# The same normalisation in another order of steps, and new slots around it, in a gated linear-attention and Fourier-mixing kernel

## The chip, the cores and the metric

The kernel runs on one core of a Trainium2 chip. The metric is the device time of one execution in microseconds (us). TensorE (PE) multiplies matrices, VectorE (DVE) and ScalarE (ACT) do the element-wise work, GpSimd (POOL) and SyncE (SP) mostly issue transfers (DMAs). Each of the five engines has its own queue of instructions and works it off in order.

## The reference, cut to what matters

x has 2048 rows and 576 columns; there are 32 heads of 18 columns.

```python
S, D, H, Dh = 2048, 576, 32, 18
g = sigmoid((x * gate_w).sum(-1, keepdims=True))
q, k, v = the three parts of x @ wqkv, by heads
phi = lambda t: where(t > 0, t + 1, exp(t)) + 1e-6
kv  = einsum("bhsd,bhse->bhde", phi(k), v)
z   = einsum("bhsd->bhd", phi(k))
num = einsum("bhqd,bhde->bhqe", phi(q), kv)
den = einsum("bhqd,bhd->bhq", phi(q), z)[..., None] + 1e-6
a   = (num / den) joined over heads, @ wo
b   = dft_seq_re @ (x @ dft_hid_re.T) - dft_seq_im @ (x @ dft_hid_im.T)
out = g * a + (1 - g) * b
```

## The kernel before

All products are made in pairs of numbers: a rounded part ("hi", written by ACT, `hi_of`) and what the rounding left ("lo", the remainder, a subtraction by DVE, `lo_of`), so that one float32 product is three matmuls. Rows are in 16 tiles of 128. The large products go by a seven-product scheme on 2 x 2 blocks. It needs sums of the blocks of each operand, the "forms", seven per operand: the class `Left` (L357) makes the forms of eight pieces of x, numbers 0 to 7, and of x's last columns, number 8 (`NP`), called x's rest. A `Left` loads its raw blocks through POOL's queue after an instruction named by the caller (`begin_after`); its generator `make` (L376) then does, one part at a time, two sums and two more sums (DVE), two roundings (ACT), and the two remainders (DVE), and `store` (L394) puts the forms into DRAM through POOL's queue, for the later stages. `store_rest` (L399) stores x's rest in six transfers through SP's queue. Some pieces are stored and loaded again (`load_forms`, `load_rest_q`); those in the dictionary `here` are used where they were made.

The stages, by the profile's times:

- *K*, to 65 us: features of k, by tile, into the 16 buffers `acc` of 128 x 576.
- *xg*, 65.3 to 130.8: phi(k) times x, in 5 chunks `c` of 4 quarters, 20 steps of 24 matmuls (18 or fewer in the last chunk). x comes in by SP through a ring of four buffers (`xg_load`), is rounded by ACT and its remainder made by DVE a step ahead (`xg_next`). `zacc` sums phi(k) over the tiles; `z_chain` and `z_sum` make z of it, `zb`. The right factors of the q product (`wq_pieces`), the forms of x's piece 6 and of x's rest, and the stores fill the engines beside it: `plan` (L728) names loads by step, `works`, `aside` and `part` (L715 to L726) hand out what is ready, one part a step.
- *q*, 130.8 to about 197: 56 slots of 7 matmuls (`q_slot`, L925). A slot is one of the seven products (`q` = 1, 6, 5, 7, 2, 4, 3) of one piece of x (`p`); pieces go in pairs, and the four pairs are `QUADS = (6, 2), (3, 4), (0, 5), (7, 1)`; a "quad" has 14 slots. Each piece gives the features of two tiles: ACT's exponentials go out with a later slot, DVE's sums (`acc`) with the slot after that. Between slots `kv_step(4)`, `build_kv` and `build_m` make M, the product of kv and wo by heads, in five groups `mf` of 126 rows; `move_m` (L858) shifts its rows to tiles of 128 with 14 transfers on SP (`mraw`, `mrest`), and `split_m` (L878) makes their rounded and remaining parts in two halves. The pieces 0, 7 and 1 of x are loaded and their forms made in this stage; the others are there or loaded (piece 6 is made and stored in the xg stage). The table `plan` (L979) says behind which slot each of these steps stands.
- *Normalisation* (`normalise`, L784): for each pair of the 16 q tiles, `pz` = (acc + EPS) x zb, its sums by head `den`, den + EPS, the reciprocal, then acc = (acc + EPS) x den and a copy of its last 64 columns twice (`twice`), all on DVE. It is a generator of four parts a pair, so 32 in all; `norms` hands them out: 8 parts in the q stage, the rest in the next stage.
- *q'M*, about 197 to 273: for each of the 16 tiles in order, 5 transposes (`transposed`, L814) into banks, from which ACT and DVE make `qs`; 28 matmuls with M (L209); ACT copies the product times the gate into `acc` (L1338), and POOL stores it (`att`). In the same loop (L1331) the sums for the next stage's right factors are made (`wr_make`) and split (`make_w`), with up to two transfers each.
- Then the hidden transform of the Fourier part (273.4 to 326), the sequence transform (326 to 504), and both again for the imaginary part.

SP's order is the program's order; ACT's and DVE's orders too, from `pace()` on, and PE's in the q stage and from the first hidden product on. POOL's order is set by the scheduler. An engine that waits holds all that stands behind it in its queue.

Two pieces of code say how the normalisation is handed out and how the q stage ends:

```python
norms = (part for k in range(NT // 2) for part in normalise(k))
...
go(norms, 3 if i < 4 else 2)          # the loop over the tiles of q'M
if i < 6:
    go(wr_make)
...
if (n, s, q) == (3, 1, 4):            # slot 53 of the q stage
    nxt = transposed(0)
```

Of the kernel before, what the change touches and what calls it, by code (L numbers as in the profile page):

```python
# [136 lines left out]
def kernel(  # L137
# [219 lines left out]
    class Left:  # L357
# [41 lines left out]
        def store_rest(self):  # L399
            for k in range(3):  # L400
                for g in range(2):
                    nc.sync.dma_start(out=xrest_of[g, k], in_=self.plain.bitcast(F)[:, g, k // 2])

# [294 lines left out]
    def rest_forms():  # L698
        yield from here[NP].make()
        here[NP].store_rest()  # L700
# [4 lines left out]
    def load_rest_q(p, o):  # L705
        rests[p] = at(o, [P, 7, P], R, "xr")
        n = min(NP * 96 - p * 96, P)
        nc.sync.dma_start(out=rests[p].bitcast(F)[:n], in_=xrest[p * 96:p * 96 + n])
# [6 lines left out]
    works = [wq_pieces[0], wq_pieces[1], left_of(6)]  # L715
    aside = [rest_forms(), wq_pieces[2]]

    def work(works=works):
        while works and next(works[0], True) is True:
            works.pop(0)  # L720

    def part():
        if lefts:
            left_part()
        else:
            work()  # L726
# [15 lines left out]
    for c in range(5):  # L742
        ps = [bank(), bank()]
        passes = FULL if c < KC else FULL[:2]
        for q in range(NCU):
# [22 lines left out]
            part()  # L768
            if step > 4:
                work(aside)  # L770
# [5 lines left out]
        part()  # L776
    tick()
    while works or aside:
        work()
        work(aside)  # L780
# [3 lines left out]
    def normalise(k):  # L784

        d = at(dens.next(), [P, 2, H], F, "den")
        for i in range(2):
            pz = at(pz_ring.next(), [P, D], F, "pz")
            nc.vector.scalar_tensor_tensor(pz, acc[2 * k + i], EPS, zb, op0=ALU.add, op1=ALU.mult)  # L789
            nc.vector.tensor_reduce(out=d[:, i], in_=pz.rearrange("p (h d) -> p h d", d=DH),  # L790
                                    op=ALU.add, axis=AX.X)
            yield
        nc.vector.tensor_scalar(d, d, EPS, None, op0=ALU.add)
        nc.vector.reciprocal(out=d, in_=d)
        for i in range(2):
            a = acc[2 * k + i].rearrange("p (h d) -> p h d", d=DH)
            nc.vector.scalar_tensor_tensor(a, a, EPS,
                                           d[:, i].unsqueeze(2).to_broadcast([P, H, DH]),
                                           op0=ALU.add, op1=ALU.mult)
            o = 2 * k + i  # L800
            o = (SLOT_AT + (14336 if o < 3 else 48256) if o < 4 else T_AT + 36864) + o % 8 * 512
            twices.append(at(o, [P, 2, REST], F, "twice"))
            rest = acc[2 * k + i][:, KC * P:]
            nc.vector.tensor_copy(out=twices[-1],
                                  in_=rest.unsqueeze(1).to_broadcast([P, 2, REST]))
            yield

    twices = []
    norms = (part for k in range(NT // 2) for part in normalise(k))


# [17 lines left out]
    kvb = at(C_AT, [GW, NG, 2, GW], R, "kvb")  # L829
# [3 lines left out]
    def build_kv():  # L833
        todo = []
        for b in range(3):
            n, k = gsize(2 * b), 2 if b < 2 else 1
            ps = kv[b][:n, :2 * k * n].rearrange("p (g t d) -> p g t d", t=2, d=n)
            lo, s = (at(C_AT + 5056 + (2 * b + i) * 1024, [GW, 2, GW], F, "kvs")[:n, :k, :n]
# [19 lines left out]
    def move_m(g):  # L858
# [639 lines left out]
```

## Time and profile before

| | us |
|---|---|
| three runs | 738.11, 740.44, 740.64 |
| median | 740.44 |
| the profiled execution | 739.57 |
| its span in the profile | 737.9 |
| PE busy in the span | 721.8 |
| DVE busy in the span | 602.6 |
| ACT busy in the span | 328.2 |

The span runs from the first to the last instruction that the profile shows; all times of rows are from its start. In the rows of the prediction a line number such as L189 is that of the helper that issued the instruction (L179 `hi_of`, L189 `lo_of`, L199 `add`, L209 `run`), and `out<-in` gives the program's names of the operands. xN is the number of instructions in a row. A bracket gives the time that the engine was idle ahead of the row and what ended it. A row of a stretch "A:B" gives its length, then the busy time and count of PE, of PE's weight loads (PEld), DVE, ACT and POOL, the mean granted clock of PE (1.00 is full speed), the busy share of the DMA engines, and GB/s.

### The profile page before, as it was taken

How to read it: one execution, taken by the hardware profiler on the slowest of the kernel's cores; microseconds unless marked ns; L12 is line 12 of the kernel's file. 1: busy time of each engine (PE TensorE's matmuls, PEld its weight loads, DVE VectorE, ACT ScalarE, POOL GpSimd, SP SyncE). 2: the span in 40 equal slices, each digit the busy share in tenths (PEclk: the TensorE clock that was granted, in tenths of full speed). 3: DMA queues.
4: the chain of work that ended last, by engine and by line, in shares of the span. 5: the costliest groups of instructions: out<-in, count | busy, mean ns of one | idle time of the engine just before them, and what ended most of it. 6: DMA issues, size and time to landing. Idle time of an engine off the chain costs nothing.

```text
span 737.9 us, 13710 instructions
## 1 busy us (share of the span) xinstructions
PE 721.8 (98%) x5390; PEld 717.3 (97%) x5390; DVE 602.6 (82%) x1004; ACT 328.2 (44%) x498; POOL 50.6 (7%) x90
## 2 busy tenths in 40 slices
PE   9999999998888999999999999999999999999997
PEld 9999999998888999999999999999999999999997
DVE  5799886668989937979999899866889987787884
ACT  6897455656633544535333333312535333233230
POOL 1111221100031110000000010000000000000000
PEclk9999999999999999999999999999999999999999
DMA  7374889972259829363457476889964444444440
GB/s 252 116 274 167 310 254 365 391 257 88 101 202 330 332 81 366 117 210 120 148 183 251 152 269 200 275 293 398 389 225 147 151 135 161 150 141 158 149 151 33
DMA packets 52037, 156.66 MB, mean 212 GB/s; under 512 B 6205, under 2 KB 8669, under 8 KB 50949
## 3 DMA queue, kind: packets, MB, share of 16 engines
q1 hardware_dynamic: 43700, 119.65, 47.6%
q0 software_dynamic: 7984, 35.73, 13.1%
q8 instruction: 43, 0.70, 0.4%
q10 hardware_dynamic: 288, 0.41, 0.2%
q14 instruction: 22, 0.17, 0.1%
HBM read 117.80 MB, written 36.49 MB: 209 GB/s over the span
## 4 chain that ended last, share of the span: by engine, by line
PE 80%; DVE 12%; DMA 4%; ACT 2%; issue 1%; SPq 0%; POOL 0%; DVEq 0%; ACTq 0%
PE bank L1276 44%; PE bank L1121 14%; PE bank L209 11%; PE bank L751 6%; DMA craw<-in_xg_dram 2%; PE bank L905 2%; PE bank L570 2%; DVE c L189 1%; ACT xb L179 1%; DVE den L790 1%; DVE sum L199 1%; DVE xb L189 1%; DVE pz L789 1%; DMA wraw<-in_wk_dram 1%; DMA craw<-in_cr_dram 1%
## 5 line engine op out<-in xcount | busy, mean ns | idle before, releaser
L1276 PE MATMUL bank<-fh,c 128*128 128x288 f32 x1792 | 355.4, 295 | 0.1
L1276 PEld LDWEIGHTS bank<-fh,c 128*128 128x128 f32 x1792 | 286.2, 188 | 0.4 <-DVE c L189 0.4
L1276 PE MATMUL bank<-fl,c 128*128 128x288 f32 x896 | 263.2, 294 | 0.0
L179 ACT ACTIVATE c<-craw 128x1792 fp32r<-128x1792 f32 (+1 forms) x84 | 121.6, 1448 | 190.9 <-DVE craw L199 168.1
L1276 PEld LDWEIGHTS bank<-fl,c 128*128 128x128 f32 x896 | 168.7, 188 | 0.0
L189 DVE TENSOR_TENSOR c<-craw,c 128x1792 fp32r<-128x1792 f32 (+4 forms) x86 | 141.9, 1652 | 6.5 <-ACT c L179 6.4
L199 DVE TENSOR_TENSOR craw<-craw 128x256 f32<-128x256 f32 (+1 forms) x192 | 98.3, 512 | 21.7 <-DMA craw<-in_ci_dram 12.8
L1121 PE MATMUL bank<-wf,xf 128*128 128x288 f32 x630 | 98.4, 296 | 0.0
L1121 PEld LDWEIGHTS bank<-wf,xf 128*128 128x128 f32 x630 | 89.9, 189 | 0.0
L209 PE MATMUL bank<-mw,qs 128*128 128x288 f32 x448 | 65.5, 304 | 6.1 <-DVE qs L189 6.0
L209 PEld LDWEIGHTS bank<-mw,qs 128*128 128x128 f32 x448 | 61.6, 192 | 7.6 <-DVE qs L189 7.5
L751 PE MATMUL bank<-pk,c 128*128 128x288 f32 x448 | 61.8, 297 | 0.3 <-ACT c L179 0.3
L751 PEld LDWEIGHTS bank<-pk,c 128*128 128x128 f32 x448 | 60.0, 188 | 1.1 <-ACT c L179 0.5
L209 PE MATMUL bank<-wd,xs 128*128 128x288 f32 (+1 forms) x336 | 44.7, 295 | 0.0
L209 PEld LDWEIGHTS bank<-wd,xs 128*128 128x128 f32 x336 | 44.6, 188 | 0.0
L199 DVE TENSOR_TENSOR ys<-bank,ys 128x288 f32<-128x288 f32 x63 | 28.8, 456 | 17.3 <-PE bank L1276 14.3
L189 DVE TENSOR_TENSOR fl<-fl,fh 128x864 fp32r<-128x864 f32 (+1 forms) x32 | 34.6, 1092 | 6.8 <-ACT fh L179 5.2
L179 ACT ACTIVATE fh<-fl 128x864 fp32r<-128x864 f32 (+1 forms) x32 | 29.8, 949 | 16.2 <-DVE fl L199 16.2
L1338 ACT ACTIVATE acc<-bank,gate 128x288 f32<-128x288 f32 x32 | 16.0, 501 | 40.6 <-PE bank L209 40.5
L1121 PE MATMUL bank<-wf,xr 96*128 96x288 f32 x112 | 33.3, 297 | 0.0
L199 DVE TENSOR_TENSOR ys<-ys,bank 128x288 f32<-128x288 f32 x47 | 21.2, 450 | 14.0 <-PE bank L1276 13.4
L905 PE MATMUL bank<-wb,xb 128*128 128x288 f32 x168 | 28.1, 304 | 3.6 <-ACT sum L946 3.0
(129 smaller groups left out, 776.1 us busy)
## 6 DMA issues: line engine op xcount, KB each, us to landing
xf<-xm SPq DMA_DIRECT2D x54, 512.0 KB, 9.2
craw<-in_cr_dram SPq DMA_DIRECT2D x32, 512.0 KB, 3.7
craw<-in_ci_dram SPq DMA_DIRECT2D x32, 512.0 KB, 4.0
xr<-xr SPq DMA_DIRECT2D x21, 448.0 KB, 8.5
xm<-xb POOLq DMA_DIRECT2D x8, 1024.0 KB, 5.1
xm<-xb POOLq DMA_DIRECT2D x8, 768.0 KB, 5.8
craw<-in_xg_dram SPq DMA_DIRECT2D x20, 256.0 KB, 5.0
xf<-xm SPq DMA_DIRECT2D x18, 256.0 KB, 9.1
```

What stands on the lines that cost most here:

```text
L179: return nc.scalar.activation(dst, src, AF.Copy, bias=bias)
L189: nc.vector.tensor_tensor(out=dst, in0=src, in1=hi, op=ALU.subtract)
L199: nc.vector.tensor_tensor(out=dst, in0=a, in1=b, op=op)
L209: nc.tensor.matmul(ps, a, b, start=(n == 0), stop=(n == len(pairs) - 1))
L570: nc.tensor.matmul(ps[i], x[:, i * P:(i + 1) * P], wkt.row(h, j), start=(c == 0 and n == 0), stop=(c == KC and n == 1))
L751: nc.tensor.matmul(ps[h][:, :HALF], t[:, a, k], pk[s][:, b, half(h)], start=(s == 0 and n == 0), stop=(s == NT - 1 and n == len(passes) - 1))
L789: nc.vector.scalar_tensor_tensor(pz, acc[2 * k + i], EPS, zb, op0=ALU.add, op1=ALU.mult)
L790: nc.vector.tensor_reduce(out=d[:, i], in_=pz.rearrange("p (h d) -> p h d", d=DH), op=ALU.add, axis=AX.X)
L905: nc.tensor.matmul(ps, a, b, start=(start and n == 0), stop=(stop and n == len(ops) - 1), skip_group_check=True)
L1121: nc.tensor.matmul(ps, a, b, start=(start and n == 0), stop=(n == len(ops) - 1), skip_group_check=True)
L1276: nc.tensor.matmul(ps[q], c[x][:, l, k], factors[p](y, f), start=(p == 0 and i == 0), stop=(p == NP - 1 and i == 2))
L1338: done.append(nc.scalar.activation(acc[i][:, half(h)], ps[:, :HALF], AF.Copy, scale=gate[:, t:t + 1]))
```

## The change

1. *Normalisation.* `normalise` is one generator over all pairs. A part has either a `pz` (ahead of the first one of a pair the reciprocal of the pair before), or a scale of the pair before, a reduce of this pair, and the copy of the tile just scaled. den + EPS goes from DVE to ACT. There are 36 parts: 10 in the q stage, and from then on two for each tile of q'M, one ahead of the next tile's transposes and one behind the product.
2. *xg stage.* A string table `turns` says at which step which generator has a part. x's rest is stored one transfer a part, not six in a row. Two tiles are added to `zacc` per step, so that z is made at step 6 and 8 instead of 10 and 12. x's piece 6 is loaded at step 6 instead of 10, and its forms are made but not stored there. The second and third piece of wq are loaded at step 8. The forms of piece 2 are loaded at step 14 instead of 13.
3. *q stage.* `plan` goes by slot number. The raw blocks of piece 7 are loaded at slot 0 instead of 14 (M's working buffers lie elsewhere, `KV_AT`, to make room), those of piece 0 at slot 2 instead of 5. The forms of 7 come at slots 10 to 17, of 0 at 14 to 24, of 1 at 33 to 38. `split_m` is at slots 30, 31, 45, 46. Groups 0 and 1 of M move through POOL's queue (5 of the 14 transfers), and the loads of the forms of piece 5 and of the rests 7 and 1 go there too. The forms of piece 6 are stored behind slot 28. `load_two` takes turns between pieces 3 and 4. In the third quad one product 1 (of the fourth) instead of two stands ahead of product 4, and tile 0 is transposed behind slot 51 instead of 53.
4. *q'M.* `wr_make` at tiles 0 and 3 to 6 instead of 0 to 5; `make_w` at 7, 8, 9, 10, 11, 12, 14 instead of 6, 7, 8, 9, 10, 12, 14.

The arithmetic and the matmuls are the same.

```diff
@@ store_rest
                     nc.sync.dma_start(out=xrest_of[g, k], in_=self.plain.bitcast(F)[:, g, k // 2])
+                    yield
@@ xg stage
-    works = [wq_pieces[0], wq_pieces[1], left_of(6)]
-    aside = [rest_forms(), wq_pieces[2]]
...
+    turns = dict(p=rest_forms(), a=wq_pieces[0], b=wq_pieces[1], c=wq_pieces[2], x=left_of(6, False))
+    turn = {4: "p", 5: "p", 6: "p", 7: "p", 8: "pap", 9: "pa", 10: "pax", 11: "pxa", 12: "paxc",
+            13: "pcbx", 14: "xbc", 15: "bc", 16: "b", 17: "b"}
     plan = {
         2: [lambda: begin_left(NP, ACC_AT)],
-        7: [lambda: go(wq_pieces[1])],
-        8: [lambda: go(wq_pieces[2])],
-        10: [z_chain, lambda: begin_left(6, ACC_AT + 22784)],
-        12: [z_sum, lambda: load_wo(2)],
-        13: [lambda: load_forms(2, ACC_AT + 8448, nc.gpsimd)],
-        14: [lambda: load_wo(3)],
+        6: [z_chain, lambda: begin_left(6, ACC_AT + 22784)],
+        8: [z_sum, lambda: go(wq_pieces[1]), lambda: go(wq_pieces[2])],
+        12: [lambda: load_wo(2)],
+        14: [lambda: load_forms(2, ACC_AT + 8448, nc.gpsimd), lambda: load_wo(3)],
...
-            for i in ((4, 5), (6, 7))[step] if step < 2 else (step + 6,):
+            for i in (2 * step + 4, 2 * step + 5):
                 if i < NT:
                     add(zacc, zacc, acc[i])
@@ normalisation
-    def normalise(k):
...
+    def normalise():
+        held = None
+        for k in range(NT // 2 + 1):
+            more = k < NT // 2
+            if held is not None:
+                nc.vector.reciprocal(out=held, in_=held)
+            if more:
+                d = at(dens.next(), [P, 2, H], F, "den")
+            for i in range(2):
+                if more:
+                    pz = at(pz_ring.next(), [P, D], F, "pz")
+                    nc.vector.scalar_tensor_tensor(pz, acc[2 * k + i], EPS, zb,
+                                                   op0=ALU.add, op1=ALU.mult)
+                yield
+                if held is not None:
+                    scale(2 * k - 2 + i, held[:, i])
+                if more:
+                    nc.vector.tensor_reduce(out=d[:, i], in_=pz.rearrange("p (h d) -> p h d", d=DH),
+                                            op=ALU.add, axis=AX.X)
+                    if i:
+                        nc.scalar.activation(d, d, AF.Copy, bias=EPS)
+                if held is not None:
+                    nc.vector.tensor_copy(*copies.pop())
+                yield
+            held = d
@@ q stage
-    kvb = at(C_AT, [GW, NG, 2, GW], R, "kvb")
+    KV_AT = T_AT + 66048
+    kvb = at(KV_AT, [GW, NG, 2, GW], R, "kvb")
...
-    def move_m(g):
+    def move_m(g, queue=nc.sync):
...
-    load_forms(3, T_AT + 37376)
     load_rest_q(4, T_AT + 108928)
-    load_forms(4, T_AT + 51712)
-    works += [left_of(k, False) for k in (0, 7, 1)]
+    load_two((3, T_AT + 37376), (4, T_AT + 51712))
...
+        0: [lambda: begin_left(7, T_AT + 94592)],
+        2: [lambda: kv_step(4), lambda: begin_left(0, SLOT_AT)],
+        4: [build_kv],
...
+        13: [lambda: load_forms(5, T_AT + 66048, nc.gpsimd)],
+        15: [lambda: load_rest_q(0, SLOT_AT + 40320), lambda: load_rest_q(5, SLOT_AT + 43904)],
+        18: [lambda: move_m(2), lambda: move_m(0, nc.gpsimd), lambda: move_m(3)],
+        19: [lambda: move_m(4), lambda: move_m(1, nc.gpsimd), lambda: begin_left(1, T_AT)],
+        28: [lambda: here[6].store(slice(0, 4), done[-1]),
+             lambda: here[6].store(slice(4, 7), done[-1])],
+        30: [spread],
+        31: [lambda: load_rest_q(7, T_AT + 80384, nc.gpsimd),
+             lambda: load_rest_q(1, T_AT + 108928, nc.gpsimd)],
+        44: [lambda: here[7].store(slice(0, 4), done[-1]),
+             lambda: here[7].store(slice(4, 7), done[-1])],
     }
+    for k, what in ((7, (10, 11, 13, 15, 17)), (0, (14, 16, 18, 20, 24)), (1, (33, 34, 35, 36, 38)),
+                    (None, (25, 27, 29, 41, 43, 45, 47, 48, 49, 52)), ("m", (30, 31, 45, 46))):
...
-            if (n, s, q) == (3, 1, 4):
+            if k == 51:
                 nxt = transposed(0)
@@ q'M
     for i, t in enumerate(seq):
         qs = nxt
+        go(norms)
         if i + 1 < NT:
             nxt = transposed(i + 1)
...
         nc.gpsimd.dma_start(out=att[t], in_=acc[i])
+        go(norms)
         tick()
-        go(norms, 3 if i < 4 else 2)
-        if i < 6:
+        if i == 0 or 2 < i < 7:
             go(wr_make)
...
-        for k, j in enumerate((6, 7, 8, 9, 10, 12, 14)):
+        for k, j in enumerate((7, 8, 9, 10, 11, 12, 14)):
```

More of the change, by code (lines that the diff above doesn't have):

```diff
@@ L767 @@
                 f()
-            part()
-            if step > 4:
-                work(aside)
+            left_part()
+            for k in turn.get(step, ""):
+                go(turns[k])
             step += 1
@@ L775 @@
             lo_later(gt[:, 1, half(h)], ps[h][:, :HALF], gt[:, 0, half(h)])
-        part()
     tick()
-    while works or aside:
-        work()
-        work(aside)
+    for f in turns.values():
+        go(f, 9)
     pz_ring = Ring(T_AT + 40960, D * 4, 4)
-    def normalise(k):
[L786 to L806, printed above, removed]
@@ new lines, in scale @@
+    def scale(t, d):
+        a = acc[t].rearrange("p (h d) -> p h d", d=DH)
+        nc.vector.scalar_tensor_tensor(a, a, EPS, d.unsqueeze(2).to_broadcast([P, H, DH]),
+                                       op0=ALU.add, op1=ALU.mult)
+        o = (SLOT_AT + (14336 if t < 3 else 48256) if t < 4 else T_AT + 36864) + t % 8 * 512
+        twices.append(at(o, [P, 2, REST], F, "twice"))
+        rest = acc[t][:, KC * P:].unsqueeze(1).to_broadcast([P, 2, REST])
+        copies.append((twices[-1], rest))
@@ L812 @@
+    twices, copies = [], []
+    norms = normalise()
     qs_ring = Ring(T_AT + 50176, XS, 2)
@@ L871, in move_m @@
             if c < KC:
-                nc.sync.dma_start(out=mraw[p:p + k, c], in_=src)
+                queue.dma_start(out=mraw[p:p + k, c], in_=src)
             else:
-                nc.sync.dma_start(out=mrest[p:p + k], in_=src)
-                nc.sync.dma_start(out=mrest[REST + p:REST + p + k], in_=src)
+                queue.dma_start(out=mrest[p:p + k], in_=src)
+                queue.dma_start(out=mrest[REST + p:REST + p + k], in_=src)
             row += k
```

90 lines of the change are left out of this document (29 added, 61 removed).

## The prediction

> **What bounds the kernel now.** I read the page first, then the stretches by stage, then the waits and the order in time of TensorE (PE), and last VectorE (DVE) where PE waited for it.
>
> ```profile
> span 737.9 us, 13710 instructions
> ...
> PE 721.8 (98%) x5390; PEld 717.3 (97%) x5390; DVE 602.6 (82%) x1004; ACT 328.2 (44%) x498; POOL 50.6 (7%) x90
> ```
>
> PE sets the time. The table by stage (bounds, length, busy us of PE, PEld, DVE, ACT, POOL, granted clock, DMA share, GB/s) says where PE is not full:
>
> ```profile
> 65.30:130.80 65.50, 65.17 (x494) 64.39 (x493) 53.50 (x94) 34.04 (x54) 12.57 (x20) 1.00 0.84 285
> 130.80:198.90 68.10, 61.89 (x444) 60.17 (x442) 52.04 (x110) 41.33 (x95) 6.56 (x10) 0.97 0.60 219
> 198.90:273.40 74.50, 70.30 (x520) 69.02 (x521) 60.29 (x122) 32.97 (x78) 13.50 (x25) 0.98 0.61 230
> 273.40:326.00 52.60, 52.60 (x395) 52.60 (x394) 40.88 (x79) 22.30 (x39) 1.12 (x2) 1.00 0.59 211
> ```
>
> The rows are the xg stage, the q stage, the q'M stage and the first hidden product. Only the second and third have idle PE, and their clock is below 1.00. The change touches just the first three, and the matmuls stay the same; so what can be won is what these two lose. What PE needs there comes from the chain of waits (start, duration, count):
>
> ```profile
> 236.46 0.44 PE bank L821 x4
> ...
> 240.71 0.44 PE bank L821 x4
> ...
> 265.99 7.42 PE bank L209 x56
> ...
> 273.41 52.60 PE bank L1121 x392
> ```
>
> The q stage has 56 slots of 7 matmuls, 392 like the last row's: 52.6, a slot 0.94. Its 40 short matmuls (kv_step, build_m) are about 5.0 at the same 0.13 each, the transposes of tiles 0 and 1 about 1.1. In q'M a tile with its transposes lasts 240.71 - 236.46 = 4.25: 14 x 4.25 and the last two tiles' 7.42 make 66.9. Sum 125.6; the stages last 68.1 + 74.5 = 142.6. **Lost: 17.0.** PE in order of time (the bracket is idle before the row, and its releaser):
>
> ```profile
> 168.95 0.96 PE L905 MATMUL bank<-wb,xf 128*128 128x288 f32 x6
> ...
> 173.08 1.75 PE L905 MATMUL bank<-wb,xb 128*128 128x288 f32 x6 [3.04 <-ACT sum L946]
> ...
> 198.96 5.66 PE L209 MATMUL bank<-mw,qs 128*128 128x288 f32 x28 [1.96 <-DVE qs L189]
> ...
> 215.54 3.98 PE L209 MATMUL bank<-mw,qs 128*128 128x288 f32 x28 [0.76 <-DVE qs L189]
> ...
> 221.91 3.97 PE L209 MATMUL bank<-mw,qs 128*128 128x288 f32 x28 [1.85 <-DVE qs L189]
> ...
> 227.82 3.99 PE L209 MATMUL bank<-mw,qs 128*128 128x288 f32 x28 [1.39 <-DVE qs L189]
> ```
>
> Five stalls: 9.0. Two are followed by slow matmuls: six in 1.75 against 0.96 at 173.08, and the next six alike (1.6 together); 28 in 5.66 against 3.98 at 198.96 (1.7). The clock shows it:
>
> ```profile
> 170.00:175.00 5.00, 1.96 (x9) 1.92 (x9) 4.79 (x10) 3.32 (x9) 0.39 (x1) 0.82 0.34 115
> ...
> 200.00:205.00 5.00, 5.00 (x30) 5.00 (x28) 4.67 (x10) 2.42 (x6) 0.00 (x0) 0.66 0.00 0
> ```
>
> So 12.3 of the 17.0 is in five places, 4.7 in gaps of 0.6 and less. In all five DVE is late: at 173.08 ScalarE (ACT) waited on DVE in its own order.
>
> **The normalisation.** DVE in order of time:
>
> ```profile
> 196.22 1.20 DVE L915 SCALAR_TENSOR_TENSOR acc<-e,sum 128x288 f32<-128x288 f32 x3
> ...
> 245.54 0.76 DVE L789 SCALAR_TENSOR_TENSOR pz<-acc,zb 128x576 f32<-128x576 f32 x1
> 246.34 0.76 DVE L790 TENSOR_REDUCE den<-pz 128x32 f32<-128x576 f32 x1
> 247.01 0.75 DVE L789 SCALAR_TENSOR_TENSOR pz<-acc,zb 128x576 f32<-128x576 f32 x1
> ...
> 248.46 0.88 DVE L189 TENSOR_TENSOR qs<-bank,qs 128x512 fp32r<-128x512 f32 x2
> 249.26 1.21 DVE L189 TENSOR_TENSOR wf<-wraw,wf 128x576 fp32r<-128x576 f32 x2
> 250.50 0.20 DVE L793 TENSOR_SCALAR den<-den 128x64 f32<-128x64 f32 x1
> 250.73 0.55 DVE L794 RECIPROCAL den<-den 128x64 f32<-128x64 f32 x1
> 251.31 0.76 DVE L797 SCALAR_TENSOR_TENSOR acc<-acc,den 128x576 f32<-128x576 f32 x1
> 252.11 0.23 DVE L804 COPY twice<-acc 128x128 f32<-128x128 f32 x1
> 252.25 0.75 DVE L797 SCALAR_TENSOR_TENSOR acc<-acc,den 128x576 f32<-128x576 f32 x1
> ```
>
> From start to start, pz to its own reduce is 0.80, the reduce to an independent pz 0.67. A pair of tiles costs 2 x (0.80 + 0.67) + 0.23 + 0.58 + 2 x (0.80 + 0.14) = 5.6. Alternating, each wide step costs about 0.67, the reciprocal 0.5, the copies 0.14, and the added EPS goes to ACT: 6 x 0.67 + 0.5 + 0.28 = 4.8. That frees 0.8 per pair, 6.6 in all, on DVE; it reaches the end only where DVE is late.
>
> A rule speaks against this: the Trainium skill, "VectorE: DVE Perf Modes", section "The DRAIN you can't avoid", says that the next VectorE operation never starts before the pipe is empty, so that chaining without semaphores saves nothing. By it only the 0.23 of EPS would go, and the forecast below would be about 1 us higher. This case's 0.80 beside 0.67 disagrees.
>
> **The order in q'M.** Now the first four tiles take three parts of the normalisation each, two pairs' worth piled on tiles 1 to 5, with wr's sums on top; hence the last four stalls. After the change each tile takes two parts, one ahead of qs and one behind, and wr's sums start at tile 3. Per tile DVE then has qs 0.80, pz 0.67, scale 0.67, reduce 0.67, copy 0.14, half a reciprocal 0.25: 3.2, with wr's sums or wf (1.24) up to 4.7 on two tiles and 4.4 on others, against PE's 4.25. From tile 2 on no stall: the gain is 4.0 (0.76 + 1.85 + 1.39).
>
> **The q stage.** Rows of the transfers and the moves:
>
> ```profile
> 155.82 8.47 SPq L872 DMA_DIRECT2D mraw<-mf  x12
> ```
> ```profile
> 132.09 0.54 POOL L395 DMA_DIRECT2D xm<-xb  x1 [13.35 <-DVE xb L189]
> ...
> 168.95 1.44 POOL L366 DMA_DIRECT2D xb<-in_xq_dram  x2 [15.05 <-DMA mraw<-mf]
> ```
> ```profile
> xm<-xb POOLq DMA_DIRECT2D x8, 768.0 KB, 5.8
> ...
> xb<-in_xq_dram POOLq DMA_DIRECT2D x16, 256.0 KB, 4.4
> ```
> ```profile
> 184.36 1.82 DVE L189 TENSOR_TENSOR mw<-mraw,mw 128x1152 fp32r<-128x1152 f32 x2
> ```
> ```profile
> 168.24 1.94 ACT L179 ACTIVATE xb<-xb 128x1024 fp32r<-128x1024 f32 x2 [1.31 <-DVE xb L199]
> ```
>
> The pieces of x's forms 7 and 0 come earlier and apart from the normalisation, so the stall at 173.08 (4.6 with its slow matmuls) goes. What is late next: x's forms 1. Their load waits until all of M's rows have moved: 13.1 now (168.95 - 155.82) for 14 transfers of about 0.7. After, 9 stay on SP and 5 go to POOL: 13.1 - 5 x 0.7 = 9.6. The moves start when the last features of the first quad are done, as now about 24.5 after slot 0. Loads issue at 34.1, land at 34.1 + 0.7 + 4.4 = 39.2; sums 1.5, ACT's rounding 1.94, DVE's first remainder 1.1: 43.8. Behind stands the new wait: x's forms 6, stored at 132.09 now, are stored from slot 28, and in POOL's queue that is behind the load of forms 1 and one transfer of x's rest. Features of the third quad overwrite them, so DVE waits there, with all that is queued behind it, the normalisation too: 34.1 + 1.44 + 0.55 + 1.1 + 5.8 = 43.0. Both chains end at about 44, when slot 37 began at 40.
>
> From there DVE has until c11 of the last quad 12 operations of 0.37, forms 1's second half 0.9, M's second half 1.8 and two pz, two scales, three reduces, two copies and a reciprocal (5.5): 12.6 to 13.2, hence 57. Slot 54, which needs its bank, could begin at 55.9: 1.5 late with slot 55 beside it. Then a reciprocal, a pz and four features lead to qs of tile 0 at 60.4: 0.5 late. From there to qs of tile 1 DVE holds ten features (3.7), scale, reduce, copy (1.5), pz and qs (1.5), 6.7 against 4.25: 2.5 late. These replace the 1.96. For a slow clock I add 0.8, half of what followed the present one; below it could be 0, above 1.7 twice.
>
> By the Trainium skill, "TensorE: Matmul & The Clock Gate", Part 1, the clock falls only after an idle window of some 3.4 us and returns after as long a busy one; with no stall that long the term would be 0, and the sum 0.8 lower. The trace does not hold with it: 1.96 idle at 198.96 was enough, 1.85 at 221.91 was not.
>
> **The xg stage.**
>
> ```profile
> 103.17 6.28 SPq L402 DMA_DIRECT2D xr<-xb  x6
> ...
> 117.59 3.66 PE bank L751 x24
> ```
>
> Six stores of x's rest held SP for 6.28 and with it the loads of xg; spread one to a step they hide behind 3.2 us of matmuls a step. But two zacc sums a step instead of one put 4 x 0.67 = 2.7 more on DVE in steps 2 to 5, where it is already without a pause. Cost 0 to 1.5; and forms 2, which wait for the last of the stores, now land near slot 1: 0 to 2. I take 0.5 for both, against 0.5 won; net 0.
>
> **Sum.** Left over: small gaps 3.5 of the 4.7, slots 54 and 55 1.5, tile 0 0.5, tile 1 2.5, clock 0.8: 8.8. Gain 17.0 - 8.8 = 8.2. The profiled execution took 739.57 (span 737.9 and 1.7 around it), 0.9 under the median of 740.44: **731.4**. With all new stalls gone 726; with the clock slow twice and transfers at their bounds 736. Its own range is 726 to 736.
>
> **Rivals.** *The backlog moves.* Slots 41 to 52 take seven parts of the normalisation and a half of M beside the features, 13 us of DVE in 11 us of PE. If the stalls before tile 1 add up to 8 instead of 4.5, with 2.5 of slow clock: 17.0 - (3.5 + 8 + 2.5) = 3, 736.6. For: DVE is 4.67 of 5.00 busy at 200 now. Against: x's pieces, 3.5 each, leave that stretch.
>
> *x's forms 6 stored too late.* As above, but if five moves on POOL run one after the other at 2.9 each, the store's landing goes from 43 to 48, and if it queues behind them by 7 more, to 55. Each us beyond 44 is a us of PE at slot 54. It decides from 57 on (13 us later eats all 8.2 and 4.8 of slack in the gaps); at 57, 744.5, slower. Against: the DMA share there is 0.00 to 0.34 now.
>
> *The xg stage is the bound.* DVE's remainders for c come late in steps 4 to 9, 0.5 each, and forms 2 by 1: 4 lost, 735.4. For: DVE without a pause there. Against: DVE 53.50 of 65.50 over the stage.
>
> *Nothing happens*, the normalisation being hidden anyway: the four qs waits speak against it.
>
> **Chances.** Forecast 0.62, backlog 0.18, xg 0.10, store too late 0.06, nothing 0.04. 0.5% is 3.7 us, about what can be told from no change: faster ends at 736.7, slower begins at 744.1. Faster: 0.60 of the forecast, 0.10 of the backlog, 0.08 of xg: 0.78. Slower: 0.05 of the late store, 0.02 of a backlog with both clocks slow: 0.07. Same 0.15. The range reaches from 725.5 to 737.5, which leaves out about 2 in 10, most of it above.
>
> **What would show it.** Right: no idle of 3 us on PE between ACT's sums and slot 34; no qs wait from tile 2 on; pz followed 0.67 later by an independent step; a wait of 1 to 3 at tile 1. Wrong: DVE idle in the middle of the q stage until a store of forms 6 has landed, for more than 2 us; remainders of c that PE waits for at 78 to 95; PE waiting for forms at slots 0 to 2.

## The result, and the profile after

| | us |
|---|---|
| after, four runs | 730.16, 731.25, 731.42, 731.51 |
| median after | 731.34 |
| median before, four runs | 740.54 |
| ratio of the two, 95% interval | 0.9868 (0.9824 to 0.9911) |
| the profiled execution after, its span | 731.42, 729.6 |

731.4 was forecast. The sum came out, but not by its own terms, as the stages show. The head of the page after:

```profile
span 729.6 us, 13716 instructions
PE 719.6 (99%) x5390; PEld 715.8 (98%) x5390; DVE 597.3 (82%) x996; ACT 329.6 (45%) x506; POOL 56.8 (8%) x101
```

DVE has 5.3 us less to do (602.6 before), PE is idle 10.0 us instead of 16.1. To compare stages of kernels whose slots interleave differently, I set the bounds at rows that all of them have: the first product of the xg stage, the first row behind the last kv_step, the first product with M, the first hidden product, the first product of a sequence stage. By these bounds, the table by stage before and then after (bounds, length, busy us of PE, PEld, DVE, ACT, POOL, clock, DMA share, GB/s):

```profile
65.30:135.59 70.29, 69.40 (x525) 68.29 (x524) 56.18 (x97) 35.98 (x58) 13.64 (x22) 1.00 0.86 290
135.59:198.96 63.37, 57.66 (x414) 56.28 (x412) 49.43 (x106) 39.46 (x90) 5.48 (x8) 0.97 0.56 207
198.96:273.25 74.29, 70.15 (x519) 68.87 (x519) 60.23 (x121) 32.91 (x78) 13.50 (x25) 0.98 0.61 231
```

```profile
65.19:135.50 70.31, 69.20 (x526) 68.27 (x524) 56.17 (x97) 35.76 (x58) 14.09 (x22) 1.00 0.81 274
135.50:194.17 58.67, 56.74 (x414) 56.24 (x413) 46.34 (x99) 38.41 (x88) 11.08 (x19) 0.97 0.66 243
194.17:262.82 68.65, 67.82 (x521) 67.21 (x520) 57.95 (x120) 35.44 (x87) 13.54 (x25) 1.00 0.66 250
```

The xg stage is as long as before; the q stage is 4.70 shorter, q'M 5.64. That is 10.3, where the forecast had 8.2 in the two. In the profiled executions 2.1 of it is missing again at the end: the two sequence stages took 177.80 and 181.95 before, 178.99 and 182.81 after. The control run below bears on whose those 2.1 are.

What PE still waits for after, from PE's rows in order of time (the bracket is idle ahead of the row and its releaser):

```profile
133.37 0.40 PE L913 MATMUL bank<-wb,xr 96*128 96x288 f32 x1 [0.35 <-DMA xr<-xr]
...
175.18 0.42 PE L913 MATMUL bank<-wb,xb 128*128 128x288 f32 x2
176.75 0.82 PE L913 MATMUL bank<-wb,xb 128*128 128x288 f32 x4 [1.15 <-DVE xb L189]
178.35 0.40 PE L913 MATMUL bank<-wb,xr 96*128 96x288 f32 x1 [0.79 <-DMA xr<-xr]
178.59 1.28 PE L913 MATMUL bank<-wb,xb 128*128 128x288 f32 x6
...
194.17 4.15 PE L209 MATMUL bank<-mw,qs 128*128 128x288 f32 x28
...
199.22 0.80 PE L209 MATMUL bank<-mw,qs 128*128 128x288 f32 x4 [0.35 <-ACT qs L179]
200.49 3.44 PE L209 MATMUL bank<-mw,qs 128*128 128x288 f32 x24 [0.48 <-DVE qs L189]
...
204.24 3.96 PE L209 MATMUL bank<-mw,qs 128*128 128x288 f32 x28
```

The wait of 3.04 at slot 34 is gone, and so are the 1.96 ahead of tile 0 (with the 5.66 that its matmuls took) and the three of tiles 3 to 5; tiles 2 to 15 follow each other without a wait for qs. In their place stand a wait at slot 41, 1.15 for the forms of x's piece 1 and 0.79 for its rest, and one of 0.83 at tile 1. Behind slot 41 the matmuls are slow again: from 176.75 to the regular slot at 182.92 are 6.17, of which 0.79 idle and 26 matmuls at the usual 0.134 account for 4.27, so 1.9 are slow clock. A second profiled execution of the same kernel waited 1.52 and 0.61 at that slot and lost nothing behind it; its rows stand in the last section.

### The profile page after: what moved, and what is told of

The parts are those of the page before. It is cut to its first block, busy times and chain, and to the rows that moved or that the text cites. A ratio compares the mean times of both kernels' runs of the same rounds, so it can differ in the third digit from the quotient of the medians.

```text
span 729.6 us, 13716 instructions
## 1 busy us (share of the span) xinstructions
PE 719.6 (99%) x5390; PEld 715.8 (98%) x5390; DVE 597.3 (82%) x996; ACT 329.6 (45%) x506; POOL 56.8 (8%) x101
## 4 chain that ended last, share of the span: by engine, by line
PE 76%; DVE 10%; DMA 9%; issue 2%; ACT 1%; SPq 1%; POOL 1%; DVEq 0%; POOLq 0%; ACTq 0%
PE bank L1270 41%; PE bank L1115 14%; PE bank L209 14%; DMA xr<-xr 2%; DVE c L189 2%; PE bank L913 2%; PE bank L748 2%; PE bank L571 2%; DVE craw L199 1%; DVE fl L189 1%; DMA wraw<-in_wq_rest_dram 1%; DMA craw<-in_xg_dram 1%; DMA xm<-xb 1%; DVE ys L199 1%; PE bank L828 1%
## 5 line engine op out<-in xcount | busy, mean ns | idle before, releaser
L209 PE MATMUL bank<-mw,qs 128*128 128x288 f32 x448 | 63.5, 298 | 0.8 <-DVE qs L189 0.5
L209 PEld LDWEIGHTS bank<-mw,qs 128*128 128x128 f32 x448 | 60.0, 188 | 1.4 <-DVE qs L189 0.7
L1292 ACT ACTIVATE ys<-bank 128x288 f32<-128x288 f32 x16 | 6.6, 412 | 53.2 <-PE bank L1270 53.2
```

The source lines that it names most:

```text
L209: nc.tensor.matmul(ps, a, b, start=(n == 0), stop=(n == len(pairs) - 1))
L1292: nc.scalar.activation(c11, ps[1], AF.Copy)
```

## Experiments

Each kernel is the one before or the one after with the edit shown. "Ratio" is to the kernel before on the same chip. The rows come from four sets of runs, in which the median of before was 740.54 (the first two rows), 742.48 (both kernels with another handing out, the dependent one, the chain alone), 741.37 (after again, the old slots, the rests on SP, the forms of 6 in xg) and 742.46 (the others); medians are compared within a set only, and across sets the ratios count. Stage lengths are from one profile of each kernel, by the bounds above.

| kernel | median us | ratio (95%) | xg | q | q'M | sequences |
|---|---|---|---|---|---|---|
| before, first profile | 740.54 | 1 | 70.29 | 63.37 | 74.29 | 177.80, 181.95 |
| after, first profile | 731.34 | 0.9868 (0.9824 to 0.9911) | 70.31 | 58.67 | 68.65 | 178.99, 182.81 |
| after again | 731.32 | 0.9861 (0.9838 to 0.9884) | 70.27 | 58.99 | 68.91 | 179.10, 183.00 |
| after, old handing out in q'M | 736.24 | 0.9931 (0.9906 to 0.9956) | 69.26 | 59.23 | 74.20 | 178.98, 182.51 |
| before, new handing out in q'M | 737.73 | 0.9940 (0.9920 to 0.9961) | 70.73 | 64.63 | 68.71 | 181.07, 182.85 |
| after, dependent normalisation | 731.65 | 0.9862 (0.9827 to 0.9897) | 70.03 | 59.62 | 69.25 | 179.41, 181.98 |
| before, chain alone | 740.51 | 0.9982 (0.9963 to 1.0001) | 69.72 | 62.98 | 73.75 | 179.36, 182.89 |
| after, old slots of pieces 0 and 7 | 731.03 | 0.9864 (0.9843 to 0.9885) | 69.62 | 59.37 | 68.84 | 179.00, 182.07 |
| after, rests 7 and 1 on SP | 729.33 | 0.9842 (0.9821 to 0.9863) | 70.19 | 57.41 | 68.89 | 179.29, 182.54 |
| after, all moves on SP | 736.89 | 0.9941 (0.9919 to 0.9962) | 69.26 | 65.28 | 68.88 | 179.26, 181.77 |
| after, forms of 6 stored in xg | 732.06 | 0.9872 (0.9849 to 0.9896) | 73.31 | 57.00 | 68.91 | 178.89, 182.82 |
| after, rests on SP, forms of 6 at slot 10 | 730.43 | 0.9842 (0.9819 to 0.9866) | 69.13 | 60.27 | 68.65 | 179.08, 182.75 |
| after, tile 0 transposed at slot 53 | 732.79 | 0.9875 (0.9850 to 0.9900) | 70.61 | 60.49 | 69.00 | 179.26, 182.61 |
| before, two edits | 737.35 | 0.9942 (0.9920 to 0.9963) | 71.05 | 62.35 | 70.31 | 178.81, 182.67 |

**The changed kernel again.** No edit.

> The changed kernel again, beside the others of this set: 731 to 732, and its profile shows whether the 2.1 us by which the two sequence stages took longer in the first profile (L1270, small pauses of 0.2 and less) are the change's or one execution's. Theory (they are one execution's): they differ by 1 or more between the two profiles. Rival (a different state of the transfers at the end of q'M): they are the same within 0.3.

The sequences took 179.10 and 183.00, 0.1 and 0.2 from the first profile of after: the two profiles of after agree, so the rival's number is the one met. But over all fourteen profiles the first sequence lies between 177.80 and 181.07, and 177.80 is the very execution from which the forecast started; the three other kernels made from before took 178.81 to 181.07, those made from after 178.89 to 179.41. So the 2.1 are hardly a price of the change: that execution of before was short there, and the medians of before in the three larger sets, 741.37, 742.46 and 742.48, lie above its 739.57. That is a likely reading, not a shown one: the kernel before itself has only that one profile.

**The handing out in q'M, undone in after and done alone in before.**

```diff
@@ after -> old handing out (the reverse, in before, is the new handing out alone)
         qs = nxt
-        go(norms)
...
-        go(norms)
         tick()
-        if i == 0 or 2 < i < 7:
+        go(norms, 3 if i < 4 else 2)
+        if i < 6:
             go(wr_make)
-        for k, j in enumerate((7, 8, 9, 10, 11, 12, 14)):
+        for k, j in enumerate((6, 7, 8, 9, 10, 12, 14)):
```

> The changed kernel with the handing out in q'M as before: three parts behind each of the first four tiles and two behind the others, wr's sums at tiles 0 to 5, make_w from tile 6. Theory (the spread over the tiles carries 4.0): the waits for qs at tiles 2 to 5 come back, 3 to 5 in all, 734.5 to 736.5. Rival (the chain frees enough DVE that the spread is not needed): no wait over 0.5, 731 to 732.5.

> The kernel before with the new handing out in q'M alone: one part ahead of the transposes and one behind, wr's sums at 0 and 3 to 6, make_w later. Theory: the three waits for qs at tiles 3 to 5 (0.76, 1.85, 1.39) go, the one of 1.96 and its slow clock stay: 4.0 less than the kernel before, 736 to 737.5. Rival (without the chain DVE is late all the same): less than 1.5 gained, 739 or more.

q'M is 74.20 with the old handing out and 68.71 with the new one in the kernel before; with and without the chain it makes 5.3 to 5.6. PE's rows of after with the old handing out:

```profile
210.90 3.99 PE L209 MATMUL bank<-mw,qs 128*128 128x288 f32 x28 [1.05 <-DVE qs L189]
...
216.36 3.97 PE L209 MATMUL bank<-mw,qs 128*128 128x288 f32 x28 [0.92 <-DVE qs L189]
...
222.28 7.24 PE L209 MATMUL bank<-mw,qs 128*128 128x288 f32 x52 [1.41 <-DVE qs L189]
```

The waits are those that the piled parts made before, though each part is a link of the chain now. The theory held in both. By the ratios the old handing out costs 0.6 to 0.7%, about 5, of which 3.4 are the three waits shown; in before the new one gives 4.7 by the medians, where 4.0 was expected (737.73 lies just above the 736 to 737.5 of the forecast). In that kernel's profile tile 0's 28 matmuls also took only 4.15 instead of 5.66, behind a wait of 1.41 instead of 1.96, while its q stage is 1.3 longer, with a wait of 1.82 for loaded forms at slot 11 (0.56 in before).

**The order of the steps on DVE, undone in after and done alone in before.**

```diff
@@ after -> dependent
+                    nc.vector.tensor_reduce(out=d[:, i], ...)          # right behind its pz
                 yield
                 if held is not None:
                     scale(2 * k - 2 + i, held[:, i])
-                if more:
-                    nc.vector.tensor_reduce(out=d[:, i], ...)
-                    if i:
-                        nc.scalar.activation(d, d, AF.Copy, bias=EPS)
-                if held is not None:
                     nc.vector.tensor_copy(*copies.pop())
                 yield
@@ and EPS on DVE, ahead of the reciprocal
+                nc.vector.tensor_scalar(held, held, EPS, None, op0=ALU.add)
                 nc.vector.reciprocal(out=held, in_=held)
```

> The changed kernel with each reduce again right behind its pz, each copy right behind its scale, and EPS added on DVE; slots and handing out as changed. Theory (slots and handing out carry the gain, the chain only frees 0.8 us of DVE a pair): DVE is behind only up to tile 1, where two pairs weigh 1.6 more; 0.5 to 2.5 above the changed kernel's 731.3, so 732 to 734, with the waits for qs of tiles 0 to 2 longer by 1 to 2 and none from tile 3 on. Rival (the chain itself carries the gain): DVE late at most tiles of q'M again, 736 or more. Second rival (order inside DVE is worth nothing, as the rule on the drain would have it): 731 to 731.6, and pz to its own reduce no longer than pz to another step.

> The kernel before with the normalisation as a chain, handed out as before. Theory: 0.8 of DVE freed a pair, two pairs of it where DVE is late: 1 to 2.5 gained, 738 to 739.5, the waits for qs shorter by that, the wait of 3.04 in the q stage still there. Rival (the chain carries the gain): 734 to 736. Second rival (order inside DVE is worth nothing): within 0.5 of the kernel before.

DVE in order of time, the same four steps, first in after and then in the dependent version:

```profile
187.66 0.76 DVE L791 SCALAR_TENSOR_TENSOR pz<-acc,zb 128x576 f32<-128x576 f32 x1
188.33 0.75 DVE L808 SCALAR_TENSOR_TENSOR acc<-acc,den 128x576 f32<-128x576 f32 x1
189.00 0.75 DVE L797 TENSOR_REDUCE den<-pz 128x32 f32<-128x576 f32 x1
189.66 0.22 DVE L802 COPY twice<-acc 128x128 f32<-128x128 f32 x1
```

```profile
187.25 0.76 DVE L792 SCALAR_TENSOR_TENSOR pz<-acc,zb 128x576 f32<-128x576 f32 x1
188.04 0.75 DVE L794 TENSOR_REDUCE den<-pz 128x32 f32<-128x576 f32 x1
188.71 0.75 DVE L805 SCALAR_TENSOR_TENSOR acc<-acc,den 128x576 f32<-128x576 f32 x1
189.49 0.23 DVE L799 COPY twice<-acc 128x128 f32<-128x128 f32 x1
```

From start to start: 0.67, 0.67, 0.66 in the chain; 0.79, 0.67, 0.78 where a step needs the one ahead of it. So the order does free what was forecast. It reaches the end only in small part: in the dependent version the waits for qs of tiles 0 and 1 grew (0.46 and 1.27, with 1.26 more ahead of the last slots), q and q'M together are 1.55 longer than in the first profile of after and 0.97 longer than in the second, and the ratio of the runs doesn't tell the two kernels apart: 731.65 lies under the 732 to 734 of the theory, next to the rival by which the order is worth nothing. By the rule of the Trainium skill, "VectorE: DVE Perf Modes", "The DRAIN you can't avoid", as the prediction put it, 0.79 and 0.67 would be one number; the rows say otherwise, though the times can't. The prediction left out that the same section lets a next operation that is not held start earlier; here the independent step starts 0.67 after the start of one that lasts 0.75, ahead of its end.

Alone in before the chain gave 0.2% (its interval ends at no change). The forecast there was wrong in a way that teaches something: the wait of 3.04 at slot 34, which was to stay, shrank to 0.78 and 0.41, and tile 0 waited 0.72 instead of 1.96. Little of that reached the end, because PE now came too early for piece 1's forms, at slot 39 of that kernel, and lost 1.5 more to slow matmuls behind it:

```profile
170.17 1.05 PE L917 MATMUL bank<-wb,xb 128*128 128x288 f32 x6 [0.78 <-ACT sum L958]
...
171.76 1.09 PE L917 MATMUL bank<-wb,xf 128*128 128x288 f32 x6 [0.41 <-ACT sum L958]
...
176.45 0.53 PE L917 MATMUL bank<-wb,xb 128*128 128x288 f32 x2 [0.66 <-ACT xb L179]
178.59 0.79 PE L917 MATMUL bank<-wb,xb 128*128 128x288 f32 x4 [1.60 <-DVE xb L189]
```

It also met a wait that I had not thought of: with a pair's parts in a chain, the scale of tile 1 comes later in the same slots, and its transposes waited for it.

```profile
203.10 0.66 PE L833 MATMUL bank<-ident,acc 128*128 128x128 f32 x4 [1.24 <-DVE acc L813]
```

**The slots of pieces 0 and 7.**

```diff
-        0: [lambda: begin_left(7, T_AT + 94592)],
+        14: [lambda: begin_left(7, T_AT + 94592)],
-    for k, what in ((7, (10, 11, 13, 15, 17)), (0, (14, 16, 18, 20, 24)), ...
+    for k, what in ((0, (15, 16, 17, 18, 20)), (7, (23, 24, 25, 27, 28)), ...
```

> The changed kernel with piece 7 loaded at slot 14 and the forms of 0 and 7 made in the order and slots of the kernel before (0 at 15 to 20, 7 at 23 to 28). Theory (pieces 7 and 0 coming together with the normalisation made the wait of 3.04 and its slow clock): a wait of 2 to 4 in the middle of the q stage comes back, 734.5 to 736.5. Rival (the lighter normalisation took that wait away): less than 1 more, under 732.5.

It gave no difference, 731.03, and the reason is instructive. PE's rows of this kernel:

```profile
169.32 1.05 PE L913 MATMUL bank<-wb,xb 128*128 128x288 f32 x6 [0.67 <-ACT sum L954]
...
172.33 1.05 PE L913 MATMUL bank<-wb,xf 128*128 128x288 f32 x6 [1.82 <-ACT sum L954]
```

The wait at slots 34 and 35 did come back, 2.5 of it, as the theory had it, with 1.5 of slow clock behind it. But the wait at slot 41 went: slot 41 came that much later, at 179.54, and the remainder that it needs, started by DVE at 177.12, was there. So both theory and rival fall, though the total is the rival's: the two waits are not added up, the larger counts. After the change the middle of the q stage is held up by the chain that leads to piece 1's forms; with the old slots by the older stall, at about the same price. The lighter normalisation has a share in it too: 2.5 came back here, not 3.04, and with the chain alone in before 1.2 was left.

**That chain.** In the chain of waits of after the moves of M (SP), the landing of the last one at 166.1 and the load of piece 1 in POOL's queue follow each other. From there it goes on in POOL's queue to the load of rest 1, which lands at 178.31; in the second profile it goes by the late store of the forms of 6, and with the rests on SP by piece 1's sums, roundings and remainders. So three branches start at that load. Three edits:

```diff
@@ rests on SP
-             lambda: load_rest_q(1, T_AT + 108928, nc.gpsimd)],       # and 7
+             lambda: load_rest_q(1, T_AT + 108928)],
@@ moves on SP (another kernel)
-        18: [lambda: move_m(2), lambda: move_m(0, nc.gpsimd), lambda: move_m(3)],      # and move_m(1)
+        18: [lambda: move_m(2), lambda: move_m(0), lambda: move_m(3)],
@@ forms of 6 stored in the xg stage (another kernel)
-    turns = dict(..., x=left_of(6, False))
+    turns = dict(..., x=left_of(6))
-        28: [lambda: here[6].store(slice(0, 4), done[-1]), ...
```

> The changed kernel with the loads of x's rests 7 and 1 on SP's queue instead of POOL's. Theory (the wait of 0.79 for rest 1 comes of its place in POOL's queue behind the forms of 1 and the stores of 6): that wait goes, the one of 1.15 for the forms of 1 stays, the slow clock behind them is shorter: 0.8 to 1.8 less, 729.5 to 730.5. Rival (the transfers share the same DMA engines, so that the forms of 1 come later instead): within 0.4 of the changed kernel.

> The changed kernel with all 14 moves of M on SP's queue. Theory (the q stage ends by the chain moves, load of the forms of 1, their forms, slot 41): the last move is issued 5 times 0.7 later, slot 41 waits 3.5 more, and a longer wait brings a longer slow clock: 3 to 5 more, 734 to 736.5. Rival (the transfers themselves, not their issue, set the time): under 1 more.

> The changed kernel with the forms of piece 6 stored in the xg stage when they are made, as in the kernel before, not behind slot 28. Theory (the late store costs only DVE's wait of 0.7 and 1.1 of POOL): the wait of DVE on that store goes, PE's waits in the q stage shrink by 0 to 0.8, the xg stage takes 0 to 1 more for the added writes: 730.5 to 732. Rival (the late store is what makes the wait at slot 41): both waits of PE there go with their slow clock, 3 or more less, 728.5.

The rests on SP: the wait of 0.79 is gone, the one of 1.24 for the forms of 1 stays, q is 57.41, and the median is 2.0 below that of after on the same chip (729.04 to 729.91 in four runs, against 729.27 to 732.18 in five). The forecast was 0.8 to 1.8 less. This is the lowest median here, but its lead over after is 0.2% by the ratios, and the intervals overlap. In its profile a wait of 0.80 for ACT's sum stands at slot 53 (0.50 in the second profile of after, none in the first).

The moves on SP cost more than the issue that I had counted, and by another way. POOL's rows in order of time, first after, then with the moves on SP:

```profile
156.78 2.65 POOL L880 DMA_DIRECT2D mraw<-mf  x5 [5.16 <-DVE acc L923]
166.81 1.53 POOL L366 DMA_DIRECT2D xb<-in_xq_dram  x2 [7.39 <-DMA mraw<-mf]
168.34 0.56 POOL L709 DMA_DIRECT2D xr<-xr  x1
168.88 1.12 POOL L395 DMA_DIRECT2D xm<-xb  x2
```

```profile
163.67 0.54 POOL L709 DMA_DIRECT2D xr<-xr  x1 [12.81 <-PE bank L913]
164.29 1.08 POOL L395 DMA_DIRECT2D xm<-xb  x2
165.46 0.55 POOL L709 DMA_DIRECT2D xr<-xr  x1
174.90 1.47 POOL L366 DMA_DIRECT2D xb<-in_xq_dram  x2 [8.89 <-issue]
```

The load waits for the moves in both. Without the moves in its queue the scheduler put the stores of piece 6 and the rests ahead of piece 1's load; they ran beside the last moves, whose landing took 8.28 in the chain of waits (3.85 in after), and the load went out 8.1 later. That the stores made the moves land late fits these rows; no run holds the stores back to show it. But PE stopped before that, at slot 35. ACT's rows and PE's in this kernel:

```profile
174.19 1.50 ACT L179 ACTIVATE mw<-mraw 128x1152 fp32r<-128x1152 f32 x2 [8.10 <-DMA mraw<-mf]
175.59 0.39 ACT L954 ACTIVATE sum<-bank 128x288 f32<-128x288 f32 x1
```

```profile
176.04 1.81 PE L913 MATMUL bank<-wb,xf 128*128 128x288 f32 x6 [7.06 <-ACT sum L954]
```

split_m stands at slot 30 after the change instead of 37, so ACT waits there for the last move, and behind it in ACT's order stands the copy of a bank that slot 35 needs. In after the last move lands at 166.1 and ACT gets to its rounding at 166.75 without a wait: the cover is less than 1 us. Where split_m stands and how the moves are issued belong together, then; with both, 0.7 to 0.8% by the ratios, 5 to 6 us, hangs on the 5 moves in POOL's queue, and q is 65.28 without them. The forecast's size (3 to 5) was a little short; its path, by slot 41, was not the one that was waited on.

The early store: the forecast of the total was met but for 0.06 (732.06), its parts were not. The xg stage is 3.0 longer, PE waiting 2.78 for a rest at slot 0 behind the added writes; the q stage is 1.8 shorter, where I had said 0 to 0.8. I tried to have both:

```diff
@@ rests on SP, and
-        28: [lambda: here[6].store(slice(0, 4), done[-1]), ...
+        10: [lambda: here[6].store(slice(0, 4), done[-1]), ...
```

> The changed kernel with the rests 7 and 1 on SP and the forms of 6 stored behind slot 10, between the xg stage and the loads of slot 13. Theory (the store in the xg stage cost 3 there and its place behind slot 28 costs 1.5 in the q stage; at slot 10 neither): xg stage within 0.5 of 70.3, q stage 56 to 57.5, 727 to 729. Rival (wherever the store lies, its 5 us of the transfers are taken from a load that is waited for): 729 or more.

The rival's number was met, 730.43, with waits of 0.57 and 1.61 for the forms of 1. But the q stage of 60.27 is not the price of the store: 2.8 of it are slow matmuls behind slot 41, which the profile with the rests on SP does not have, and 0.9 are the longer waits. By the ratio the two kernels are the same (0.9842 both). In each of the three places that were tried something was waited for; the best one is not shown.

**The end of the q stage.** One edit in after, two in before (the new handing out is the other):

```diff
@@ after -> slot 53
-            if k == 51:
+            if k == 53:
@@ before -> slot 51
-            if (n, s, q) == (3, 1, 4):
+            if (n, s, q) == (3, 1, 2):
```

> The changed kernel with tile 0 transposed behind slot 53 again instead of 51. Theory (the earlier transposes took away the wait of 1.96 for qs of tile 0 and the slow clock behind it): a wait of 1 to 2.5 for qs of tile 0 comes back, with 0 to 1.7 of slow clock: 732.5 to 735. Rival (the fewer and shorter steps on DVE took it away): no wait over 0.5 there, 731 to 732.

> The kernel before with two edits alone: the new handing out in q'M, and tile 0 transposed behind slot 51 instead of 53. Theory (these two places carry most of the gain): the waits for qs of tiles 0 and 3 to 5 go, the one of 3.04 in the middle of the q stage stays; 6 to 8 less than the kernel before, 733.5 to 736. Rival (at slot 51 DVE is still behind in that kernel, so that the wait moves to the slots after it): as with the first edit alone, 737 to 738.5.

At slot 53 a wait of 1.45 for qs of tile 0 came back in after, and with it the slow clock, 28 matmuls in 5.87 instead of 4.15:

```profile
196.56 5.87 PE L209 MATMUL bank<-mw,qs 128*128 128x288 f32 x28 [1.45 <-DVE qs L189]
```

q is 1.5 to 1.8 longer, with a wait of 1.09 for ACT's sum at slot 53 as well; q'M is as long as in after, since tile 1 no longer waits, and the runs give 0.1% (inside the intervals). In before, q with the earlier transposes is 2.3 shorter than with the new handing out alone, 62.35, but only 0.9 of that is tile 0's wait (0.47 instead of 1.41); the rest is a shorter wait for loaded forms at slot 11 and fewer slow matmuls behind the stall of 3.04. q'M grew by 1.6: DVE was still behind, and the waits came after tile 0:

```profile
198.63 4.13 PE L209 MATMUL bank<-mw,qs 128*128 128x288 f32 x28 [0.47 <-DVE qs L189]
...
204.94 3.99 PE L209 MATMUL bank<-mw,qs 128*128 128x288 f32 x28 [0.57 <-DVE qs L189]
...
226.28 0.63 PE L821 MATMUL bank<-ident,acc 128*128 128x128 f32 x4 [0.35 <-DVE acc L797]
```

My theory that these two places carry most of the gain is false: 737.35 is the rival's number. In before neither slot 51 (0.47 left) nor the chain (0.72 left) takes all of tile 0's wait away; in after, with more room on DVE ahead of it, none is left at slot 51, and 1.45 at slot 53.

## Why the prediction was right, point by point

- **q'M.** Right, by its steps. The three waits of tiles 3 to 5 and the slow clock at tile 0 went, and undoing the handing out gave about 5 back. Tile 1 was forecast 2.5 late and was 0.83 late; which of DVE's operations ahead of it came earlier than counted was not tried apart.
- **The q stage.** Size right by chance: the step that failed is the 4.6 for the stall. I said that the stall of 3.04 with its 1.6 of slow matmuls goes because pieces 7 and 0 come earlier. It went, and in the old slots 2.5 of it came back; but with them there the time is the same, so that the earlier slots are worth nothing by themselves. What I had worked out, both chains at 43.8 after slot 0, was near: with slot 0 at about 131.5 (three slots and a kv_step ahead of 135.50), slot 41, the first with a product of piece 1's forms, went on at 176.75, 45.2 behind it. But I set these times against slot 54 and DVE's backlog, and did not ask which slot reads piece 1's forms. It is slot 41, due at 175.18. So 3.8 of the 4.6 that I struck off stayed there (1.15, 0.79 and 1.9) in the first profile, and 2.1 in the second (1.52 and 0.61, no slow clock). Which edit carries the 4.7 (4.4 in the second profile) of this stage stays open: without the earlier slots, without slot 51 or without the chain, one at a time, it is 0.7, 1.8 and 1.0 longer than in the first profile.
- **The terms that made up for it.** In the first profile slots 54 and 55 (1.5) and tile 0 (0.5) have no wait, tile 1 has 1.7 less; the gaps that I kept at 3.5 are about 2. Left over in the two stages are 6.7 of the 17.0, not 8.8. The late slots are not free of it, though: the second profile has 0.50 at slot 53, and other versions 0.6 to 1.3 at slots 53 or 55.
- **The slow clock.** 0.8 was put; 1.9 behind slot 41 and 0.2 at tile 0 came in the first profile, and in the second nothing behind slot 41.
- **The chain.** 0.8 freed on DVE a pair, reaching the end only where DVE is late: right, and no more than 1.6 in the profiles. DVE's busy time fell by 5.3 in all, and by 4.0 against the dependent version, where 6.6 had been put.
- **The xg stage.** Net 0: right as a sum, 70.29 and 70.31. Which of its two terms is right was not tried apart, and between profiles of kernels with the same xg stage it varies by up to 1.5.
- **x's forms 6 stored late.** The place was right: DVE waits at that point, 0.72 until 177.41, 45.9 after slot 0 where I had worked out 43.0. As a rival to a faster time it did not come; the store costs the q stage 1.8, and it would have cost xg 3.0.
- **The base.** The profiled execution of before was the fastest in the first sequence stage of all fourteen. Against its 739.57 the gain is 8.2; by the ratios, 0.9868 and 0.9861, it is 9.8 to 10.3, as in the stages. That the forecast meets 731.34 so closely is two errors of about 2 that cancel.
- **Queues.** The moves on POOL I had priced at 3.5 of issue; without them the q stage is 6.3 to 6.6 longer. Two steps failed: split_m's move to slot 30, of which I had costed no wait on ACT, and POOL's order, which changes when the moves leave it.

## What to carry to other kernels

When a stall is struck off, write down for each late operand the slot that reads it first, not only the end of the stage: two waits in a row on the same engine don't add up, and the one behind takes over (here with the old slots, and with the chain alone). Spread optional work evenly over the tiles of a loop, one part ahead of and one behind the step that is waited for; here that was worth 0.6% with five changed lines, while a better order of the same steps on an engine that is late in a few places only was worth 0.2% (between nothing and 0.4% by its interval), since the next wait took over. What is taken out of a queue changes the order of the rest of it: look at what then goes first.

## What the runs showed of the hardware

Short idle of PE can bring slow matmuls, but whether and how long is not told by its length. Windows of after, first the first profile, then the second (length, busy us, clock as before):

```profile
175.00:180.00 5.00, 3.07 (x18) 2.60 (x17) 3.81 (x7) 3.64 (x10) 0.00 (x0) 0.90 0.44 161
180.00:185.00 5.00, 5.00 (x31) 5.00 (x31) 4.78 (x11) 3.26 (x8) 0.73 (x2) 0.75 0.01 3
```

```profile
177.88 0.80 PE L913 MATMUL bank<-wb,xb 128*128 128x288 f32 x4 [1.52 <-DVE xb L189]
179.28 0.40 PE L913 MATMUL bank<-wb,xr 96*128 96x288 f32 x1 [0.61 <-DMA xr<-xr]
```

```profile
175.00:180.00 5.00, 2.87 (x20) 2.40 (x19) 3.60 (x8) 3.87 (x8) 0.00 (x0) 1.00 0.62 247
180.00:185.00 5.00, 5.00 (x39) 5.00 (x38) 5.00 (x12) 3.92 (x11) 0.52 (x1) 1.00 0.01 3
```

Two waits of 1.15 and 0.79 in 2.7 us were followed by 1.9 lost, and at the same slot of the same kernel 1.52 and 0.61 by none, with the granted clock at 1.00 throughout. The stall at slot 34, 3.04, 3.01 and 3.04 in before, with the new handing out and with the two edits, was followed by 1.6, 2.7 and 1.4 lost. Elsewhere, one wait of 1.45 (tile 0 at slot 53) by 28 matmuls in 5.87; but 1.41 at 222.28 with the old handing out by none, 52 matmuls in 7.24, and 1.85 at 221.91 in before by none. A wait of 7.06 cost little more than the short ones: three slots from 176.04 to 181.21, 5.17 where 2.81 is usual, so 2.4; I had expected a longer wait to bring a longer slow clock. So a difference of 1 to 3 us between single profiled executions can be this alone. The Trainium skill, "TensorE: Matmul & The Clock Gate", Part 1, asks for an idle window of some 3.4 us before the clock falls; these runs do not agree. Its window is said to run freely, so that where a wait falls in it may decide; no run here shows that.
